# Weights one at a time through all banks, the attention's tenth product behind z2 row 7, and no marking matmuls

## The chip, the cores and the metric

One core of a Trainium2 chip runs the kernel. The metric is device time in microseconds (us), taken as the median of several executions. One further execution was taken with the hardware profiler; rows of the profile come from that one alone.

## The reference

```python
def reference(A_x, A_wqkv, A_wo, B_x, B_w_in, B_w_sp, B_b_sp, B_w_out):
    x = A_x                                   # 1 x 2048 x 512, fp32
    xn = _layernorm(x, axis=-1)
    s = _A_ref(xn, A_wqkv, A_wo)              # attention: 32 heads of 16, window of 8 keys, dilation 2, then @ wo
    g = _silu(_B_ref(xn, B_w_in, B_w_sp, B_b_sp, B_w_out))
    return x + s * g

def _B_ref(x, w_in, w_sp, b_sp, w_out):       # Fh = 896
    z = _gelu(jnp.einsum("bsd,df->bsf", x, w_in))
    z1 = z[..., :Fh]
    z2 = _layernorm(z[..., Fh:], axis=-1)
    g = jnp.einsum("ts,bsf->btf", w_sp, z2) + b_sp[None, :, None]   # w_sp is 2048 x 2048
    return jnp.einsum("bsf,fd->bsd", z1 * g, w_out)
```

## The kernel before

Every fp32 matrix product is made of three matmuls on operands that are split into a high and a low part: high x high, high x low, low x high. A split (`split`, L194) is one copy on ACT (L195, the high part) and one subtraction on DVE (L197, the low part). The 2,048 rows stand in 16 tiles of 128; "row j" below is such a tile.

The stages on TensorE (PE) are, in this order: the qkv product; z1; z2 (`z2_half`, L725, two halves of each row: 512 columns with h = 0 and 384 columns with h = 1, each in a PSUM bank of its own); the mixing product with `w_sp` (`block_product`, L848, in fourteen parts named m1a, m1b, m2a, ... in Strassen's manner, from sums and differences of blocks); the product with `w_out` (L1067 to L1069, tile b); and the product of the attention with `wo` (the same lines, tile s).

A mixing part with the letter a or b runs in one half of the eight PSUM banks: `banks[0, f]` for a, `banks[1, f]` for b, with three or four banks f each. It runs over eight weight blocks s. For a bank and a block, `three` (L823) issues three matmuls of 512 columns. Blocks are taken in pairs: within a pair, bank 0 takes its three matmuls of block s0 and its three of block s0 + 1, then bank 1 takes the same two blocks, and so on. The weights (`wsp_...` from `w_sp`, `ws_...` from sums that were stored before) are loaded into one of four raw buffers, and split into one of eight pairs of weight buffers. m1a uses z2 rows 0 to 7 as the stationary operand, m1b the same rows, and m2a and m2b use rows 8 to 15.

The first parts, m1a and m1b, are not opened by a matmul that overwrites. ACT writes a bias into each bank first (`seed`, L842) and the matmuls add to it. For that, the whole bank has to have been marked as written by a matmul. The banks of m1a were last used by 512-column halves of z2. Those of m1b, `banks[1, f]`, were last used by the 384-column halves of rows 6, 14, 7 and 15; so `second_seeds` (L981) first issues four 512-column matmuls that mark them (L984), one for each bank, and then the four seeds. It is called after blocks 4 and 5 of m1a.

z2 rows come in pairs i and i + 8. After both halves of both rows have gone through Gelu on ACT (L733), `z2_stats` (L738) takes their statistics (DVE L742, L743 and L745, then POOL L746 and L748), and `z2_normal` (L752) normalises a row on ACT (L754) and splits it. `combine` (L759) makes differences and sums of a row pair on DVE (L767), splits one and stores the others. Rows 7 and 15 are the last pair.

DVE also carries the whole attention, in one fixed order (`line`, L537): 32 steps, each with a score product (L573), a reduction (L580), a weighted product (L620, collected in `sums_of`) and some folds (L638 to L646); a first fold runs on POOL (L633). Its output goes to memory (`o_d`), and `load_o` (L803) reads it back for the last stage, in four groups of four tiles (o_0 to o_3).

The order of the instructions on each engine is made ahead of time by a scheduler that simulates the run; every engine then works strictly in that order. Manual dependencies that add no wait (NOSYNC) only constrain that order. One such holds `sums_of[9]`, the tenth weighted product, behind the low part of weight block 6 of m1a (L864); as the attention is one line, all that follows it there waits too.

Of the kernel before, what the change touches and what calls it, by code (L numbers as in the profile page):

```python
# [13 lines left out]
AF = mybir.ActivationFunctionType  # L14
# [5 lines left out]
FH = F // 2  # L20
FQ = FH // 2
H, DH, W, DIL = 32, 16, 8, 2
NT = S // P
# [3 lines left out]
CT = 512  # L27
NC = S // CT
JC = NT // NC
HT = NT // 2  # L30
F3 = 3 * P
ODD = 3
# [20 lines left out]
NOSYNC = mybir.DependencyInfo(mybir.DependencyClass.NoSync, mybir.DependencyReason.DATA)  # L53
# [4 lines left out]
def kernel(  # L58
# [13 lines left out]
    nc = tc.nc  # L72
    pins = [True]
    lows, highs, sums_of = [], [], []

    def pin(ins):
        return tc.keep_in_program_order(ins) if pins[0] else ins
# [35 lines left out]
    mvz = const.tile([P, NT, 2], F32, name="mvz")  # L113
    nmz = const.tile([P, NT], F32, name="nmz")
# [5 lines left out]
    def xn_at(j):  # L120
        return planes[:, FB - KB :, j, 0], planes[:, FB - KB :, j, 1]

    def z2_at(j):
        return planes[:, :, j, 0], planes[:, :, j, 1]

    def half(i):
        return BIG[:, i * CT : (i + 1) * CT]
# [16 lines left out]
    def blocks(t, n=KB):  # L144
        return t.rearrange("p (k q) -> p k q", k=n)
# [9 lines left out]
    def mm(name):  # L155
        return ps.tile([P, 512], F32, tag=f"bank{next(turn)}", name=name)
# [3 lines left out]
    def weight_pair(name):  # L160
        i = next(slot)
        return (
            wts.tile([P, 512], F32R, tag=f"whi{i}", name=name + "h"),
            wts.tile([P, 512], F32R, tag=f"wlo{i}", name=name + "l"),
        )

    def fetch(src, n, name):
        raw = raws.tile([P, 512], F32, tag="raw", name=name + "r", bufs=RAW)
        pin(nc.sync.dma_start(raw[:, :n], src))
        return raw  # L170

    def side_pair(name):
        return [wts.tile([P, CT], F32R, tag=f"w{n}", name=name + n) for n in "hl"]

    def prep(src, n, name, raw=None, pair_=None):
        if raw is None:
            raw = fetch(src, n, name)
        hi, lo = pair_ or weight_pair(name)
        split(hi[:, :n], lo[:, :n], raw[:, :n])
        return hi, lo  # L180
# [13 lines left out]
    def split(hi, lo, src):  # L194
        first_ = pin(nc.scalar.activation(hi, src, AF.Copy))  # L195
        highs.append(first_)
        lows.append(pin(nc.vector.tensor_tensor(lo, src, hi.bitcast(F32), op=ALU.subtract)))  # L197
        return first_
# [48 lines left out]
    rows = {}  # L247
# [45 lines left out]
    first = []  # L293
# [401 lines left out]
    for f in range(FB):  # L695
        pair_ = side_pair("w1_last") if f == FB - 1 else None
        wh, wl = prep(w_in1[:, f, :], KB * P, f"w1_{f}", pair_=pair_)
        for c in range(NC):
            pz = mm(f"z1_{f}_{c}")
            for k in range(KB):  # L700
                cc = slice(k * P, (k + 1) * P)
                xh, xl = [planes[:, FB - KB + k, c * JC : (c + 1) * JC, a] for a in range(2)]
# [5 lines left out]
            zt = zp[:, c % 2]  # L708
# [8 lines left out]
    HALF = (slice(0, 512), slice(512, FH))  # L717
    WID = (512, FH - 512)
    w2 = {
        (k, h): prep(w_in2[:, k, HALF[h]], WID[h], f"w2_{k}_{h}")  # L720
        for h in range(2)
        for k in range(KB)
    }

    def z2_half(j, h, zt):  # L725
        xh, xl = xn_at(j)
        pz = mm(f"z2_{j}_{h}")[:, : WID[h]]
        for k in range(KB):
            wh, wl = [w[:, : WID[h]] for w in w2[k, h]]
            nc.tensor.matmul(pz, xh[:, k], wh, start=k == 0, stop=False)  # L730
            nc.tensor.matmul(pz, xh[:, k], wl, start=False, stop=False)  # L731
            nc.tensor.matmul(pz, xl[:, k], wh, start=False, stop=k == KB - 1)  # L732
        nc.scalar.activation(zt[:, HALF[h]], pz, AF.Gelu_apprx_tanh)  # L733

    def spatial_block(c, js):
        return prep(w_sp[c, js], CT, f"wsp_{c}_{js}")
# [14 lines left out]

    def z2_normal(j, zt, n):  # L752
        zh, zl = z2_at(j)
        nc.scalar.activation(zt, zt, AF.Identity, bias=nmz[:, j : j + 1], scale=mvz[:, j, 1:2])  # L754
        split(zh[:, :n], zl[:, :n], blocks(zt, FB)[:, :n])

    first_part, last_part = slice(0, F3), slice(FH - F3, FH)

# [19 lines left out]
    spatial = {(0, 0): early_pair}  # L778
    raw_z = {}
    for i in range(HT + 2):  # L780
        if i in (1, 3):
            raw_sums(1, HT - 2 + i // 2)
        if i < HT:
            raw_z[i] = [t4(f"zt_{j}").rearrange("p i t -> p (i t)")[:, :FH] for j in (i, HT + i)]
            for h in range(2):
                for j, zt in zip((i, HT + i), raw_z[i]):
                    z2_half(j, h, zt)
                if i == HT - 1 and h == 0:
                    spatial[0, 1] = spatial_block(0, 1)
        if i == 5:  # L790
            b_a = t4("b_a")
            nc.sync.dma_start(
                b_a, b_sp[0:2, :].rearrange("c t -> (c t)").unsqueeze(0).to_broadcast([P, 2 * CT])
            )
            biases = [[b_a[:, 0], b_a[:, 1]]]
        if 0 < i <= HT:
            z2_stats(i - 1, raw_z[i - 1])
        if i > 1:
            for j, zt, n in zip((i - 2, HT + i - 2), raw_z[i - 2], (ODD + 1, FB)):
                z2_normal(j, zt, n)  # L800
            combine(i - 2, raw_z[i - 2])
# [21 lines left out]
    def three(pg, z, w, start=False, stop=False, seeded=False):  # L823
        for i, (a, b) in enumerate(((0, 0), (0, 1), (1, 0))):
            nc.tensor.matmul(  # L825
                pg, z[a], w[b], start=start and i == 0, stop=stop and i == 2, skip_group_check=seeded
            )

    def z2_block(j, f):
        return [planes[:, f, j, a] for a in range(2)]  # L830
# [6 lines left out]
    banks = {}  # L837
    for n in range(8):
        a, f = n // 2 % 2, n // 4 * 2 + n % 2
        banks[a, f] = mm(f"g_{a}_{f}")  # L840

    def seed(a, f, src, scale=1.0):  # L842
        return nc.scalar.activation(banks[a, f], src, AF.Copy, scale=scale)
# [3 lines left out]

    def block_product(a, name, z, w, odd=None, start=False, stop=False, steps=()):  # L848
        for n, s0 in enumerate(range(0, HT, 2)):
            pair_ = [(s, w(s)) for s in (s0, s0 + 1)]  # L850
            for f in range(ODD):
                for s, wp in pair_:
                    three(banks[a, f], z(s, f), wp, start and s == 0, s == HT - 1, not start)
            if odd:
                for s, wp in pair_:
                    three(banks[a, ODD], odd(s), wp, False, s == HT - 1, True)
            for do in steps[n] if steps else ():
                do()

    def plain(a, c, r):  # L860
        def w(s):
            js = r * HT + s
            pair_ = spatial.get((2 * a + c, js)) or spatial_block(2 * a + c, js)
            if (a, c, js) == (0, 0, 6):  # L864
                tc.add_manual_dep(
                    sums_of[9].ins, lows[-1].ins.name, NOSYNC, reason="first weights ahead"
                )
            return pair_

        return w  # L870

# [17 lines left out]
    def odd(r):  # L889
        return lambda s: z2_block(r * HT + s, ODD)  # L890
# [88 lines left out]
            nc.sync.dma_start(biases[1][i], b_sp[2 + i : 3 + i, :].to_broadcast([P, CT]))  # L979

    def second_seeds():  # L981
        for f in range(ODD + 1):

            nc.tensor.matmul(  # L984
                banks[1, f], z2_block(0, f)[0], half(0), start=True, stop=True
            )
        for f in range(ODD + 1):
            seed(1, f, biases[1][0])

    block_product(  # L990
        0, "m1a", at(0, 0), plain(0, 0, 0), odd(0),
        steps=(
# [6 lines left out]
    def kept(a):  # L999
# [7 lines left out]

    kept(0)
    block_product(1, "m1b", at(0, 0), plain(1, 0, 0), odd(0))
    kept(1)  # L1010
    block_product(
        0, "m2a", at(1, 0), plain(0, 0, 1), odd(1),
        steps=([T3[0]], [T3[1]], [T3[2]], [T3[3]]),
# [59 lines left out]
    for i, j in enumerate(rows_of):  # L1073
        c, jj = divmod(j, JC)
# [104 lines left out]
```

## Time and profile before

| | |
|---|---|
| median of 3 executions | 695.06 us (694.0 to 696.38) |
| the profiled execution | 696.54 us |
| its span, first to last instruction | 694.8 us |
| PE busy | 686.6 us (99%) |
| DVE busy | 619.4 us (89%) |
| ACT busy | 277.7 us (40%) |
| POOL busy | 215.2 us (31%) |

A busy PE is not PE at its peak: matmuls overlap, so one lasts 389 ns while the next starts earlier. The start-to-start distance is what counts. 1.74 us of the profiled execution lie outside its span.

### The profile page before, as it was taken

The page shows a single profiled execution, that of the slowest core. Times are in us where ns is not written, and L with a number is a line of the kernel's source. Part 1 is how long each engine was busy: PE and PEld are TensorE (multiplying, and loading weights), DVE is VectorE, ACT ScalarE, POOL GpSimd, SP SyncE. Part 2 cuts the span into 40 slices and gives each one's busy share as a digit, 9 for nine tenths or more (in the row PEclk, how much of TensorE's full clock was granted, in tenths as well). Part 3 has the DMA queues.
Part 4 walks back from the last instruction along what each step waited for, and adds up shares of the span by engine and source line. Part 5 has one row for each costly group of instructions (what it writes and reads, how often), then busy time and mean ns, then how long its engine had stood idle before and what let it go on. Part 6 is the DMA issues. An engine that isn't in the chain of part 4 may idle for free.

```text
span 694.8 us, 9233 instructions
## 1 busy us (share of the span) xinstructions
PE 686.6 (99%) x3084; PEld 573.0 (82%) x3084; DVE 619.4 (89%) x866; ACT 277.7 (40%) x458; POOL 215.2 (31%) x242
## 2 busy tenths in 40 slices
PE   8999999999999999998999999999999999999998
PEld 7888888888888899986888888888888888888886
DVE  6776868999989989889999998999989999989775
ACT  4342234224424256865534544442334444211531
POOL 3104837372343322124123222223111201642320
PEclk9999999999999999999999999999999999999999
DMA  8769899969999865267899768667576692655796
GB/s 270 252 193 289 288 348 384 346 204 358 407 412 340 329 231 190 80 201 231 258 403 314 284 211 298 208 232 248 183 261 206 215 342 89 221 173 190 246 330 235
DMA packets 102223, 182.36 MB, mean 262 GB/s; under 512 B 9184, under 2 KB 45280, under 8 KB 102176
## 3 DMA queue, kind: packets, MB, share of 16 engines
q1 hardware_dynamic: 56624, 102.21, 43.6%
q0 software_dynamic: 13824, 52.24, 20.9%
q10 hardware_dynamic: 31728, 27.33, 11.7%
q8 instruction: 24, 0.39, 0.2%
q14 instruction: 23, 0.19, 0.1%
HBM read 122.42 MB, written 59.32 MB: 262 GB/s over the span
## 4 chain that ended last, share of the span: by engine, by line
PE 67%; DVE 13%; DMA 12%; ACT 3%; issue 3%; POOL 1%; SPq 1%; DVEq 0%; POOLq 0%; ACTq 0%
PE g L825 35%; PE b L1067 4%; PE b L1069 4%; PE b L1068 4%; PE qkv L387 4%; PE qkv L386 4%; PE qkv L385 4%; DMA sb<-in_w_sp 3%; PE s L1069 2%; PE s L1068 2%; PE s L1067 2%; DMA sums_d<-sb 2%; DVE zst L742 2%; DMA z_d<-z1t 1%; DVE xT L280 1%
## 5 line engine op out<-in xcount | busy, mean ns | idle before, releaser
L633 POOL TENSOR_TENSOR pv<-pv 128x1024 f32<-128x1024 f32 x29 | 69.6, 2399 | 96.2 <-DVE pv L620 85.9
L573 DVE TENSOR_TENSOR pr<-k,q 128x2048 f32<-128x2048 f32 x32 | 73.6, 2299 | 2.0 <-DMA k<-qkv_d 1.9
L620 DVE TENSOR_TENSOR pv<-v,lg 128x2048 f32<-128x2048 f32 x32 | 74.6, 2331 | 0.7
L580 DVE TENSOR_REDUCE lg<-pr 128x128 f32<-128x2048 f32 x32 | 73.0, 2281 | 0.1
L647 POOL DMA_DIRECT2D o_d<-tt x32 | 18.0, 562 | 138.9 <-DVE tt L646 103.8
L433 ACT ACTIVATE stage<-qkv 128x512 f32<-128x512 f32 x40 | 23.0, 590 | 30.8 <-DMA qkv_d<-stage 17.0
L807 POOL DMA_DIRECT2D ol<-o_d x32 | 17.7, 555 | 37.7 <-DVE BIG L197 11.1
L1078 ACT ACTIVATE bt<-b 128x512 f32<-128x512 f32 x16 | 9.4, 599 | 43.5 <-PE b L1069 39.4
L709 ACT ACTIVATE z1t<-z 128x512 f32<-128x512 f32 x28 | 15.5, 597 | 26.1 <-DMA z_d<-z1t 15.3
L280 DVE TENSOR_TENSOR xT<-xT,mr 128x512 f32<-128x512 f32 x20 | 14.9, 743 | 11.9 <-DMA mr<-mv_d 6.4
L732 PE MATMUL z<-w_0h,BIG 128*128 128x512 f32 x64 | 25.0, 391 | 0.0
L731 PE MATMUL z<-w_0l,BIG 128*128 128x512 f32 x64 | 25.0, 391 | 0.0
L730 PE MATMUL z<-w_0h,BIG 128*128 128x512 f32 x64 | 24.9, 390 | 0.0
L742 DVE BATCH_NORM_STATS2 zst<-zt 128x6 f32<-128x448 f32 x32 | 19.3, 613 | 6.1 <-ACT zt L733 6.0
L754 ACT ACTIVATE zt<-zt,nmz,mvz 128x896 f32<-128x896 f32 x16 | 17.5, 1129 | 18.0 <-POOL nmz L748 18.0
L638 DVE TENSOR_TENSOR pv<-pv 128x512 f32<-128x512 f32 x32 | 22.9, 716 | 0.0
L733 ACT ACTIVATE zt<-z 128x512 f32<-128x512 f32 (+1 forms) x32 | 15.9, 536 | 15.2 <-DMA sums_d<-sa 14.0
L732 PE MATMUL z<-w_1h,BIG 128*128 128x384 f32 x64 | 21.5, 336 | 0.0
L730 PE MATMUL z<-w_1h,BIG 128*128 128x384 f32 x64 | 21.5, 335 | 0.0
L731 PE MATMUL z<-w_1l,BIG 128*128 128x384 f32 x64 | 21.4, 335 | 0.0
L393 POOL TENSOR_TENSOR sb<-sa,sb 128x512 f32<-128x512 f32 x12 | 19.7, 1644 | 5.4 <-DMA sb<-in_w_sp 5.1
L195 ACT ACTIVATE BIG<-zl 128x512 fp32r<-128x512 f32 x20 | 12.5, 630 | 21.6 <-DVE zl L895 19.8
(478 smaller groups left out, 2296.2 us busy)
## 6 DMA issues: line engine op xcount, KB each, us to landing
qkv_d<-stage ACTq DMA_DIRECT2D x24, 512.0 KB
v<-qkv_d POOLq DMA_DIRECT2D x14, 704.0 KB, 5.4
k<-qkv_d POOLq DMA_DIRECT2D x13, 704.0 KB, 6.8
sums_d<-sa POOLq DMA_DIRECT2D x14, 512.0 KB, 7.8
sums_d<-sb POOLq DMA_DIRECT2D x14, 512.0 KB, 8.0
z_d<-z1t ACTq DMA_DIRECT2D x14, 512.0 KB
zl<-z_d SPq DMA_DIRECT2D x12, 512.0 KB
tr<-t_d SPq DMA_DIRECT2D x12, 384.0 KB
```

The lines of the kernel that those rows point to most:

```text
L573: line(nc.vector.tensor_tensor(pr, taps(ks[u], j0), qb.unsqueeze(1).to_broadcast([P, W, NJ * CS]), op=ALU.mult))
L580: line(nc.vector.tensor_reduce(lgs[u][:, j0 * HS : (j0 + NJ) * HS].rearrange("p i w -> p w i"), pr.rearrange("p w (i d) -> p w i d", d=DH) ...
L620: line(nc.vector.tensor_tensor(pv.rearrange("p w (i d) -> p w i d", d=DH), taps(vs[u], j0).rearrange("p w (i d) -> p w i d", d=DH), lgs[u] ...
L633: eng.tensor_tensor(pv[:, 0:4], pv[:, 0:4], pv[:, 4:8], op=ALU.add)
L730: nc.tensor.matmul(pz, xh[:, k], wh, start=k == 0, stop=False)
L731: nc.tensor.matmul(pz, xh[:, k], wl, start=False, stop=False)
L732: nc.tensor.matmul(pz, xl[:, k], wh, start=False, stop=k == KB - 1)
L742: nc.vector.bn_stats(st[:, h], zt[:, h * FQ : (h + 1) * FQ])
L825: nc.tensor.matmul(pg, z[a], w[b], start=start and i == 0, stop=stop and i == 2, skip_group_check=seeded)
L1067: nc.tensor.matmul(pp[:, cols], hi, wh, start=k == 0, stop=False)
L1068: nc.tensor.matmul(pp[:, cols], hi, wl, start=False, stop=False)
L1069: nc.tensor.matmul(pp[:, cols], lo, wh, start=False, stop=k == n - 1)
```

## The change

- `block_product` takes the weight blocks one at a time: for each block s, all banks get their three matmuls before the next block begins. The number and the kinds of matmuls stay the same.
- `second_seeds` loses its four marking matmuls. In their place the first matmul of the 384-column half of rows 6, 7, 14 and 15 writes all 512 columns of its bank. For this the first weight block of that half (`w2_0_1`) is loaded and split with 512 columns instead of 384, the half's result stands in the last 384 columns of its bank, and the other matmuls remain 384 wide.
- The order constraint on `sums_of[9]` moves from the low part of weight block 6 of m1a to the low part of z2 row 7.
- A new order constraint on ACT puts the normalisation of row 15 behind the high part of row 7.

```diff
@@ w2 and z2_half
     w2 = {
-        (k, h): prep(w_in2[:, k, HALF[h]], WID[h], f"w2_{k}_{h}")
+        (k, h): prep(
+            w_in2[:, k, slice(FH - CT, FH) if (k, h) == (0, 1) else HALF[h]],
+            CT if (k, h) == (0, 1) else WID[h],
+            f"w2_{k}_{h}",
+        )
         for h in range(2)
         for k in range(KB)
     }
 
     def z2_half(j, h, zt):
         xh, xl = xn_at(j)
-        pz = mm(f"z2_{j}_{h}")[:, : WID[h]]
+        bank = mm(f"z2_{j}_{h}")
+        pz = bank[:, CT - WID[h] :]
         for k in range(KB):
-            wh, wl = [w[:, : WID[h]] for w in w2[k, h]]
-            nc.tensor.matmul(pz, xh[:, k], wh, start=k == 0, stop=False)
+            wh, wl = [w[:, CT - WID[h] :] if k == 0 else w[:, : WID[h]] for w in w2[k, h]]
+            if k == 0 and j % HT >= HT - 2:
+                nc.tensor.matmul(bank, xh[:, k], w2[k, h][0], start=True, stop=False)
+            else:
+                nc.tensor.matmul(pz, xh[:, k], wh, start=k == 0, stop=False)
             nc.tensor.matmul(pz, xh[:, k], wl, start=False, stop=False)
             nc.tensor.matmul(pz, xl[:, k], wh, start=False, stop=k == KB - 1)
@@ z2_normal
-        nc.scalar.activation(zt, zt, AF.Identity, bias=nmz[:, j : j + 1], scale=mvz[:, j, 1:2])
+        ins = nc.scalar.activation(zt, zt, AF.Identity, bias=nmz[:, j : j + 1], scale=mvz[:, j, 1:2])
+        if j == NT - 1:
+            tc.add_manual_dep(ins.ins, highs[-1].ins.name, NOSYNC, reason="first products' row ahead")
         split(zh[:, :n], zl[:, :n], blocks(zt, FB)[:, :n])
+        if j == HT - 1:
+            tc.add_manual_dep(sums_of[9].ins, lows[-1].ins.name, NOSYNC, reason="gate rows ahead")
@@ block_product
         for n, s0 in enumerate(range(0, HT, 2)):
-            pair_ = [(s, w(s)) for s in (s0, s0 + 1)]
-            for f in range(ODD):
-                for s, wp in pair_:
+            for s in (s0, s0 + 1):
+                wp = w(s)
+                for f in range(ODD):
                     three(banks[a, f], z(s, f), wp, start and s == 0, s == HT - 1, not start)
-            if odd:
-                for s, wp in pair_:
+                if odd:
                     three(banks[a, ODD], odd(s), wp, False, s == HT - 1, True)
@@ plain
-            pair_ = spatial.get((2 * a + c, js)) or spatial_block(2 * a + c, js)
-            if (a, c, js) == (0, 0, 6):
-                tc.add_manual_dep(
-                    sums_of[9].ins, lows[-1].ins.name, NOSYNC, reason="first weights ahead"
-                )
-            return pair_
+            return spatial.get((2 * a + c, js)) or spatial_block(2 * a + c, js)
@@ second_seeds
         for f in range(ODD + 1):
-
-            nc.tensor.matmul(
-                banks[1, f], z2_block(0, f)[0], half(0), start=True, stop=True
-            )
-        for f in range(ODD + 1):
             seed(1, f, biases[1][0])
```

## Rows read from the trace of the kernel before

**Rows 1.** The page: busy time by engine; granted clock in 40 slices, tenths of full.

```profile
PE 686.6 (99%) x3084; PEld 573.0 (82%) x3084; DVE 619.4 (89%) x866; ACT 277.7 (40%) x458; POOL 215.2 (31%) x242
...
PEclk9999999999999999999999999999999999999999
```

**Rows 2.** Busy us by stage: stretch, length, PE, PEld, DVE, ACT, POOL, clock, DMA, GB/s.

```profile
295.13:342.27 47.14, 45.03 (x197) 36.59 (x197) 44.87 (x70) 28.00 (x47) 12.77 (x14) 1.00 0.70 221
342.27:570.94 228.67, 228.67 (x1010) 189.35 (x1009) 220.94 (x300) 94.39 (x156) 52.41 (x51) 1.00 0.76 262
```

**Rows 3.** PE's waits between 290 and 330 us: total, times, longest.

```profile
PE g L825 <- ACT g L843: 1.9, 1, 1.9
PE g L825 <- ACT BIG L195: 0.2, 1, 0.2
```

**Rows 4.** PE in order of time, m1a and m1b: start, duration, engine, line, operation.

```profile
290.94 0.33 PE L730 MATMUL z<-w_1h,BIG 128*128 128x384 f32 x1
...
295.13 0.39 PE L825 MATMUL g<-wsp_0h,BIG 128*128 128x512 f32 x1
...
311.49 1.07 PE L984 MATMUL g<-BIG 128*128 128x512 f32 x4
312.39 0.39 PE L825 MATMUL g<-wsp_6h,BIG 128*128 128x512 f32 x1
...
317.17 0.50 PE L825 MATMUL g<-wsp_0h,BIG 128*128 128x512 f32 x1 [1.90 <-ACT g L843]
...
324.48 0.50 PE L825 MATMUL g<-wsp_7h,BIG 128*128 128x512 f32 x1 [0.21 <-ACT BIG L195]
...
342.30 0.39 PE L825 MATMUL g<-wsp_8h,BIG 128*128 128x512 f32 x1
```

**Rows 5.** ACT in order of time: last Gelu, m1b's seeds, rows 7 and 15.

```profile
303.82 0.47 ACT L733 ACTIVATE zt<-z 128x384 f32<-128x384 f32 x1
...
313.99 0.64 ACT L195 ACTIVATE wsp_3h<-wsp_3r 128x512 fp32r<-128x512 f32 x1 [5.03 <-DMA wsp_3r<-in_w_sp]
...
316.53 2.14 ACT L843 ACTIVATE g<-b_bh 128x512 f32<-128x512 f32 x4
321.22 2.16 ACT L754 ACTIVATE zt<-zt,nmz,mvz 128x896 f32<-128x896 f32 x2 [2.54 <-POOL nmz L748]
...
323.81 1.88 ACT L195 ACTIVATE BIG<-zt 128x512 fp32r<-128x512 f32 x3
```

**Rows 6.** DVE in order of time: attention between row 7's steps.

```profile
304.04 2.29 DVE L620 TENSOR_TENSOR pv<-v,lg 128x2048 f32<-128x2048 f32 x1
306.24 2.28 DVE L580 TENSOR_REDUCE lg<-pr 128x128 f32<-128x2048 f32 x1
...
309.29 0.62 DVE L742 BATCH_NORM_STATS2 zst<-zt 128x6 f32<-128x448 f32 x1
...
313.22 2.28 DVE L573 TENSOR_TENSOR pr<-k,q 128x2048 f32<-128x2048 f32 x1
...
327.36 2.15 DVE L197 TENSOR_TENSOR BIG<-zt,BIG 128x512 fp32r<-128x512 f32 x3
```

**Rows 7.** POOL in order of time: the reciprocal root for rows 7 and 15.

```profile
318.82 1.68 POOL L746 TENSOR_TENSOR mvz<-mvz,nhalf 128x2 f32<-128x2 f32 x1 [1.83 <-DVE mvz L745]
```

**Rows 8.** DVE's longest waits between 350 and 660 us: total, times, longest.

```profile
DVE ws_4l L197 <- ACT ws_4h L195: 3.6, 2, 2.3
DVE o_0l L197 <- ACT o_0h L195: 2.2, 1, 2.2
```

**Rows 9.** The attention's last tile: its low part on DVE, its first use on PE.

```profile
679.59 0.69 DVE L197 TENSOR_TENSOR o_3l<-ol,o_3h 128x512 fp32r<-128x512 f32 x1 [3.30 <-ACT o_3h L195]
...
682.07 0.39 PE L1069 MATMUL s<-BIG,o_3l 128*128 128x512 f32 x1
```

**Rows 10.** The weight block with the shortest lead: low part, first use.

```profile
392.05 0.68 DVE L197 TENSOR_TENSOR ws_5l<-ws_5r,ws_5h 128x512 fp32r<-128x512 f32 x1
...
395.33 0.39 PE L825 MATMUL g<-ws_5l,BIG 128*128 128x512 f32 x1
```

## The prediction

> **What bounds the kernel now.** I read the page first: TensorE (PE) is busy for 686.6 of 694.8 us, and its granted clock is full in each of the 40 slices [rows 1]. So the time is that of PE's stream of matmuls and its gaps, and only removed matmuls or closed gaps can count. Next I looked for the gaps by stage. From 342 to 571 us PE is busy for the whole stretch: 1,010 matmuls in 228.67 us, 0.2264 us each [rows 2]. That is the price of a dense 512-column matmul. The stretch before it, m1a with m1b, has 2.1 us in which PE is idle [rows 2]. Then the waits: PE waits twice here, 1.9 us for the seeds of m1b and 0.2 us for a high part of z2 [rows 3]. Last, the order of the matmuls around these waits [rows 4]: after block 6 of m1a PE does not go on to block 7, which needs row 7. It waits for m1b's seeds and begins m1b, and comes back to block 7 at 324.48. So row 7 is late, and the seeds that would fill in for it are late too.
>
> Why they are late is seen on the other engines. The last Gelu of rows 7 and 15 is done at 304.29 [rows 5]. Then DVE takes up the attention at 304.04: the tenth weighted product, the reduction, a score product (2.3 us each) and folds [rows 6]. Row 7's statistics stand between these (309.29), POOL has its root at 320.5 [rows 7], ACT normalises rows 7 and 15 from 321.22 and copies from 323.81 [rows 5], and the low parts come from 327.36 [rows 6]. The seeds ran at 316.53, four microseconds after the marking matmuls on which they wait. They stood on ACT behind copies of m1b's later weights, one of which waited 5 us for its transfer [rows 5].
>
> **What the dense stream would give.** From 295.13 to 342.30, 47.17 us, PE issues 192 weighted and four marking matmuls [rows 4]. At 0.2264 these take 44.4. So the two waits cost **2.8 us**: 2.1 idle, and the rest around them, as a matmul after a wait lasts 0.50 instead of 0.39 and the next one starts later [rows 4].
>
> **Part by part.**
> - *The marking matmuls go.* Four, from 311.49 to 312.39: **0.90 us** off PE's stream [rows 4]. The seeds lose their wait for PE; they then need only the Gelu that empties the last bank (304.29 [rows 5]) and the bias.
> - *Narrow halves wider.* The last 24 narrow matmuls take 290.94 to 295.13, 0.175 us each [rows 4]; a wide one takes 0.226. Four of them: **0.2 us** added to the stream. The wider first weight adds about a third to one load, one copy and one subtraction early in z2; a 512-column copy and subtraction last 0.64 and 0.68 us in all [rows 5, 10]. PE does not wait there; without that cover it would be below 0.2 us.
> - *The tenth product behind row 7's low part.* DVE is in order, so everything of the attention waits with it; POOL's fold and the loads of the next keys, queries and values wait for those in turn. Row 7's chain after its last Gelu: statistics 0.62 [rows 6], POOL's root 1.68 [rows 7], one normalisation (half of 2.16) and one copy (a third of 1.88) [rows 5], one subtraction 0.7 [rows 6]; with some 1.1 for the small steps between them (an estimate from POOL's 320.50 and ACT's 321.22 [rows 5, 7], 0.7 for one handover, and a little for the other) that is 5.8 us, so 310.1 at the earliest. At the latest: from 304.04 to the low parts at 327.36 are 23.3 us, and DVE is hardly idle (44.87 of 47.14 us busy [rows 2]). Five large attention steps lie in it, the three shown and one more product and reduction of the same length, 11.4 us [rows 6]; all the rest, 11.9 us at most and with wsp_6's low part among it, done first would end near 315.2, when that 0.7 is taken off. PE needs row 7's high part after 84 dense matmuls from 295.13, at 314.2, and its low part two matmuls later, at 314.6. So the cost of what is left of the wait lies between 0 and 0.6 us. I take 0.3, as the late end assumes that the scheduler lets nothing of row 7 go ahead.
> - *What DVE loses.* The work that goes ahead is work that stood between the attention's steps anyway, so the attention is moved, not lengthened, by as much as DVE idles for row 7's chain: between 0 and 5.8 us, were there nothing else to do. I take 1, as some 11 us of other work lie there.
> - *Row 15 behind row 7.* In the trace ACT normalises both rows in one go, then copies [rows 5]. Now row 7's copy goes between: 1.1 us earlier for row 7, 0.6 later for row 15, which is first used by block 7 of m2a, over 40 us on. Nothing.
> - *One block at a time.* The same matmuls. An odd block is needed nine matmuls later than before with four banks (2.0 us), an even block's buffer is free nine earlier. The shortest lead that I found between a low part and its use is 2.6 us (392.73 to 395.33 [rows 10]); this order lengthens leads. Against it: m1b's second to fourth bank are needed three matmuls (0.68 us) after one another instead of six; four seeds take 2.14, or 0.53 each [rows 5], so they keep up. At the end of a part the first bank is complete 9 instead of 18 matmuls ahead, but the next part works in the other four banks, so 72 or 96 matmuls, 16 to 22 us, pass before it is needed. Nothing.
>
> Sum: 0.9 - 0.2 + 2.8 - 0.3 = 3.2; I take **3.1 us**, leaving 0.1 for the restart. The ceiling is 0.9 - 0.2 + 2.8 = 3.5. The profiled execution of 696.54 (span 694.8 and 1.74 around it) would become 693.4. It lies 1.5 above the median of 695.06, and for the median I forecast **692.0 us**.
>
> **A rule against the reordering.** The row first: through 342 to 571 us PE changed banks every six matmuls, some 170 times, with no idle time at a granted clock of 1.00, the 2.4 GHz level [rows 2]. The Trainium skill, "TensorE: Matmul & The Clock Gate", section "A second HAM failure mode: psum-queue depth-cycling", tells of a kernel that cycled through banks and had so many tiny idle times between groups that the clock fell back again and again; by that rule three matmuls a bank would cost time in all fourteen parts. The trace so far speaks against it. It is the last rival below.
>
> **The rivals.**
> 1. *The attention becomes the end.* The low part of the attention's last tile is done at 680.28 and used at 682.07: 1.8 us to spare [rows 9]. If PE comes 3.1 us earlier and the attention does not, 1.3 us are given back: 693.3. For it: DVE is 97% busy from 342 to 571 [rows 2]. Against: DVE waits for ACT later on, 5.8 us in three waits alone [rows 8], on copies that wait for buffers or queues that PE frees; those waits absorb a DVE that is late.
> 2. *Row 7 isn't what it waits for, or the scheduler places it as late as before.* Then only the markers count, 0.9 - 0.2: 694.4. For it: what else stood between the Gelu and the root on DVE. Against: the attention's share of that stretch is half of it.
> 3. *Slower: the attention starts too late and nothing absorbs it.* If DVE idles through all of row 7's chain, the tenth product begins at 310.1 instead of 304.04, and if the later waits are set by transfers, the last tile comes 5.8 us later: 1.8 are spare, so the end moves by 4.0, to 699.1. It decides from a slip of 1.8 us plus what the waits of [rows 8] absorb (5.8): below 1.8 never, above 7.6 always.
> 4. *The clock falls with the bank changes.* No row here has the lower level; were a tenth of the 1,200 weighted matmuls to take twice 0.2264, it would be 27 us more: 722.
>
> **How the numbers follow.** Forecast 0.54 (691.0 to 692.9; it includes a gain at the ceiling); attention at the end 0.16 (692.6 to 694.3); no cure for row 7 0.11 (694.4); attention far too late 0.16 (696 to 699); the clock 0.02; an unrelated change of the scheduler's order for the worse 0.01. A measurement of this kernel can tell about 0.3%, 2.1 us, from no change: below 692.97 is faster, above 697.15 slower. The forecast and a tenth of the first rival's higher gains give faster 0.56; the rest of rivals 1 and 2 and the mild half of rival 3 make 0.32; slower 0.12. The range 690.8 to 696.6 leaves out the worse part of rival 3 and the clock; its low end is the ceiling (691.6) less the 0.8 by which a median of such runs can lie low.
>
> **What would show it.** Right: no marking matmuls; PE without a wait from 295 to about 338.8, where m2a begins (342.3 minus 3.5); block 7 of m1a directly behind block 6, row 7's copy on ACT before 314; the seeds of m1b on ACT before 314; the tenth product right behind row 7's low part at 309 to 315; the last tile's low part about 3 us earlier; DVE's later waits shorter. Wrong: PE waiting for `o_` parts after 640 (rivals 1 and 3), a wait for a high part of z2 (rival 2), or a granted clock below 1.00 (rival 4). The sum would be wrong from its start if the scheduler's order in the stages behind m2a brought PE new waits where it has none today.

## The result: 0.33% slower, and where the time went

The changed kernel takes 698.22 us in the median (693.67 to 702.03, 22 runs), the kernel before 695.95 us in the same series (694.0 to 698.45, 22 runs). The ratio is 1.0033, with a 95% interval of [1.0018, 1.0047]: slower by a little, but clear of the noise, where 692.0 us and faster was forecast. The profiled execution of the changed kernel took 698.9 us, with a span of 697.0.

These are the two lines of the changed kernel's page that answer to [rows 1]. PE is as busy as before with four matmuls fewer, and the granted clock is still full.

```profile
PE 686.5 (98%) x3080; PEld 571.7 (82%) x3080; DVE 619.6 (89%) x866; ACT 275.9 (40%) x458; POOL 214.7 (31%) x242
PEclk9999999999999999999999999999999999999999
```

Stage windows of the changed kernel (columns as in [rows 2]): m1a with m1b, which had 2.1 us of idle PE before, is dense now. The stretch from 500 to 580 us, part of a stretch without any idle time before, has lost 3.9 us.

```profile
295.20:342.30 47.10, 47.04 (x208) 38.62 (x207) 41.93 (x67) 28.60 (x49) 11.43 (x12) 1.00 0.71 222
342.30:500.00 157.70, 157.70 (x697) 130.59 (x696) 150.05 (x196) 60.02 (x102) 40.46 (x39) 1.00 0.76 261
500.00:580.00 80.00, 76.13 (x331) 61.29 (x330) 77.01 (x112) 32.84 (x56) 12.58 (x13) 1.00 0.72 238
```

PE's waits in the changed kernel (line, what released it: total, times, longest), those behind the start. The two of [rows 3] are gone; three new ones stand in the last mixing part and the output product, for weights:

```profile
PE g L837 <- DVE ws_0l L197: 1.8, 1, 1.8
PE b L1068 <- ACT wout_5h L195: 1.2, 1, 1.2
PE b L1069 <- DVE wout_2l L197: 0.8, 1, 0.8
```

The order around row 7 is what was asked for. ACT, then DVE, in order of time: the seeds run at 307.58 instead of 316.53 [rows 5], row 7 has its high part at 313.14, DVE its low part at 313.88, and the tenth product comes right behind, at 314.48 instead of 304.04 [rows 6].

```profile
307.58 2.16 ACT L855 ACTIVATE g<-b_bh 128x512 f32<-128x512 f32 x4 [1.25 <-DMA b_bh<-in_b_sp]
...
311.58 1.14 ACT L762 ACTIVATE zt<-zt,nmz,mvz 128x896 f32<-128x896 f32 x1 [0.87 <-POOL nmz L756]
...
313.14 0.62 ACT L195 ACTIVATE BIG<-zt 128x512 fp32r<-128x512 f32 x1
```

```profile
313.27 0.69 DVE L197 TENSOR_TENSOR wsp_3l<-wsp_3r,wsp_3h 128x512 fp32r<-128x512 f32 x1 [1.31 <-ACT wsp_3h L195]
313.88 0.68 DVE L197 TENSOR_TENSOR BIG<-zt,BIG 128x512 fp32r<-128x512 f32 x1
314.48 2.28 DVE L620 TENSOR_TENSOR pv<-v,lg 128x2048 f32<-128x2048 f32 x1
```

The largest of the new waits, first on PE, then on DVE, then on ACT. PE has its high part and waits for the low part of ws_0. ACT had made the high part from 530.67 on, so neither the transfer nor ACT is late. DVE had it right behind the 23rd product and its reduction in its order, 4.4 us of work, and reached it at 536.53. In the kernel before the 23rd product ran at 523.34; here at 532.13.

```profile
535.38 0.39 PE L837 MATMUL g<-ws_0h,BIG 128*128 128x512 f32 x1
537.53 0.50 PE L837 MATMUL g<-ws_0l,BIG 128*128 128x512 f32 x1 [1.76 <-DVE ws_0l L197]
```

```profile
532.13 2.28 DVE L620 TENSOR_TENSOR pv<-v,lg 128x2048 f32<-128x2048 f32 x1
534.33 2.27 DVE L580 TENSOR_REDUCE lg<-pr 128x128 f32<-128x2048 f32 x1
536.53 0.95 DVE L197 TENSOR_TENSOR ws_0l<-ws_0r,ws_0h 128x512 fp32r<-128x512 f32 x1
```

```profile
530.67 0.64 ACT L195 ACTIVATE ws_0h<-ws_0r 128x512 fp32r<-128x512 f32 x1 [1.71 <-DMA ws_0r<-sums_d]
```

The same low part and its first use in the kernel before: done at 532.20, used at 538.36, a lead of 6.2 us. In the changed kernel DVE is done with it 5.3 us later (537.48), and PE would have used it 2.6 us earlier (537.53 less the wait of 1.76). Together that is 7.9 us: the lead is used up, and 1.7 us of wait remain.

```profile
531.53 0.67 DVE L197 TENSOR_TENSOR ws_0l<-ws_0r,ws_0h 128x512 fp32r<-128x512 f32 x1
...
538.36 0.39 PE L825 MATMUL g<-ws_0l,BIG 128*128 128x512 f32 x1
```

Of the other two waits, that for wout_2 is for a low part on DVE as well; that for wout_5 is for a high part on ACT, which had waited for that block's transfer.

DVE also lost time between row 7 and these waits. At 432.80 it waits 3.4 us for the high part of a stored row difference (`tr`), for whose transfer ACT had waited 3.9 us; in the second execution of the changed kernel DVE waits 3.1 us there. None of the three executions of the kernel before has this wait. Why the transfer comes late is open. ACT, then DVE:

```profile
431.92 0.85 ACT L195 ACTIVATE BIG<-tr 128x768 fp32r<-128x768 f32 x1 [3.92 <-DMA tr<-t_d]
```

```profile
432.80 0.96 DVE L197 TENSOR_TENSOR BIG<-tr,BIG 128x768 fp32r<-128x768 f32 x1 [3.42 <-ACT BIG L195]
```

Three profiled executions of the kernel before and two of the changed one (the further ones are experiments below) put this into one table. It is made from the starts of three matmuls on PE: the first of m1a, the first of m2a, the last of all.

| execution | m1a and m1b, us | m2a to the last matmul, us | together |
|---|---|---|---|
| before | 47.17 | 348.72 | 395.89 |
| before, second | 45.14 | 348.72 | 393.86 |
| before, third | 45.30 | 348.72 | 394.02 |
| changed | 43.91 | 354.15 | 398.06 |
| changed, second | 43.69 | 352.97 | 396.66 |

From m2a on, the kernel before takes the same 348.72 us three times: nothing makes its PE wait there. The changed kernel gains 1.2 to 3.5 us in m1a and m1b and loses 4.3 to 5.4 us behind them. The means differ by 2.8 us, the medians by 2.3.

### The profile page after: what moved, and what is told of

Same layout as the page of the kernel before. It is cut to its first block, busy times and chain, and to the rows that moved or that the text cites. A ratio compares the mean times of both kernels' runs of the same rounds, so it can differ in the third digit from the quotient of the medians.

```text
span 697.0 us, 9227 instructions
## 1 busy us (share of the span) xinstructions
PE 686.5 (98%) x3080; PEld 571.7 (82%) x3080; DVE 619.6 (89%) x866; ACT 275.9 (40%) x458; POOL 214.7 (31%) x242
## 4 chain that ended last, share of the span: by engine, by line
DVE 33%; PE 31%; DMA 17%; issue 13%; ACT 2%; POOL 1%; SPq 1%; DVEq 0%; ACTq 0%; POOLq 0%
DVE lg L580 5%; DVE pr L573 5%; PE qkv L385 4%; PE qkv L386 4%; PE qkv L387 4%; PE b L1068 3%; PE b L1070 3%; PE b L1069 3%; DVE BIG L197 3%; DMA tr<-t_d 3%; DVE pv L620 3%; PE s L1070 2%; PE s L1069 2%; PE s L1068 2%; DMA sums_d<-sb 2%
## 5 line engine op out<-in xcount | busy, mean ns | idle before, releaser
L740 PE MATMUL z<-w_0h,BIG 128*128 128x512 f32 x64 | 25.0, 391 | 0.0
L754 POOL TENSOR_TENSOR mvz<-mvz,nhalf 128x2 f32<-128x2 f32 x8 | 7.6, 944 | 51.3 <-DVE mvz L753 51.3
L738 PE MATMUL z<-w_0h,BIG 128*128 128x512 f32 x60 | 23.3, 389 | 0.0
L740 PE MATMUL z<-w_1h,BIG 128*128 128x384 f32 x64 | 21.5, 336 | 0.0
L552 POOL DMA_DIRECT2D k<-qkv_d x13 | 7.0, 536 | 44.5 <-DVE pr L573 44.5
```

## The experiments

The first four undo one part of the change, do one part alone, or take work off DVE. "Idle" below is DVE's idle time from 295 to 340 us: 2.3 us in the first execution of the kernel before (0.9 in each of the other two), 5.2 and 4.7 in the two of the changed kernel.

**Block pairs again (a_pairs).** The changed kernel with its blocks in pairs.

```diff
-            for s in (s0, s0 + 1):
-                wp = w(s)
-                for f in range(ODD):
+            pair_ = [(s, w(s)) for s in (s0, s0 + 1)]
+            for f in range(ODD):
+                for s, wp in pair_:
```

> The changed kernel with the weight blocks of block_product taken in pairs again; all else as changed. Theory (the attention, held behind row 7, leaves DVE with a backlog, and low parts of weights come late to PE): the order of the blocks is not the cause, so the tenth product still starts near 314 us, PE still waits 2 to 5 us for low parts between 500 and 580, and the time is 1.003 of before, near 698. Rival (taking blocks one at a time makes the scheduler put the weights' low parts later on DVE): no PE wait after 500 us, and 692 to 693.5.

Measured: 1.0014 [0.9992, 1.0036]; idle 4.1; no wait from 500 to 580 us in its profile. The shortest lead of a low part there is 1.4 us, where the changed kernel has leads of 0.0 to 0.4 at nine blocks. The late waits that the theory expected are gone, but the time of the rival isn't reached either. The profile suggests that the order of the blocks has a share in the loss together with the rest; the times do not show it, as this interval overlaps that of the changed kernel.

**The constraint back at weight block 6 (a_dep6).** The changed kernel without the hold behind row 7; row 15 stays behind row 7.

```diff
-        if j == HT - 1:
-            tc.add_manual_dep(sums_of[9].ins, lows[-1].ins.name, NOSYNC, reason="gate rows ahead")
+            if (a, c, js) == (0, 0, 6):
+                tc.add_manual_dep(sums_of[9].ins, lows[-1].ins.name, NOSYNC, reason="first weights ahead")
```

> The changed kernel with the constraint on the tenth weighted product moved back to weight block 6 of m1a; blocks one at a time, no marking matmuls and row 15 behind row 7 as changed. Theory (backlog of DVE from the held attention): the tenth product is back near 304 us, row 7 is late again and PE waits 1 to 3 us near 315 to 325, but under 0.5 us between 500 and 580; the time is 694 to 695.5, about 1 below before. Rival (order of the blocks): waits of 2 us or more between 500 and 580 stay, and the time is 697 to 699.

Measured: 1.0015 [0.9994, 1.0036]; idle 2.0, the tenth product at 302.5; row 7 costs PE only 0.26 us, but there are waits of 1.1 us for ws_6's low part at 395, 0.5 for wout_3's and 1.0 for o_3. Neither expectation holds: PE isn't held at row 7, and the gain of 1 us is not there.

**Single blocks alone (b_single).** The kernel before with only the new block order.

```diff
-            pair_ = [(s, w(s)) for s in (s0, s0 + 1)]
-            for f in range(ODD):
-                for s, wp in pair_:
+            for s in (s0, s0 + 1):
+                wp = w(s)
+                for f in range(ODD):
```

> The kernel before with one part of the change alone: weight blocks one at a time. Theory (backlog of DVE): no new wait after 330 us, within 0.3% of before, 694 to 697. Rival (order of the blocks): 2 to 5 us of new PE waits for low parts after 500 us, 698 to 701.

Measured: 1.0001 [0.9983, 1.0018]; idle 0.9; after 295 us PE waits only once, 0.3 us for o_3. By itself the new order neither gains nor costs. That the new order makes the late waits by itself is refuted.

**A lighter DVE (a_light).** The changed kernel with the reduction of steps 15 to 26 taken over half of each head's elements, about 13 us less on DVE.

```diff
-                pr.rearrange("p w (i d) -> p w i d", d=DH),
+                pr.rearrange("p w (i d) -> p w i d", d=DH)[:, :, :, : DH // 2 if 14 <= 2 * u + j0 // NJ < 26 else DH],
```

> The changed kernel with less work on DVE: in twelve of the attention's 32 steps (the 15th to the 26th) the reduction sums only half of each head, so 1.1 us is saved in each, 13 us in all (the scores of these steps are then partial sums). Theory (backlog of DVE): PE's waits between 500 and 580 shrink from 5 us to under 0.5, and the time is 691.5 to 693. Rival (order of the blocks, or anything on ACT or the transfers): the waits stay within a microsecond of 5, and the time is above 696.5.

Measured: 1.0045 [1.0024, 1.0065], no cure. The tenth product came at 315.2, idle was 6.7, and PE waited 1.8 us for ws_1's low part at 522. The windows from 430 to 565 us, of a_light and then of the changed kernel, show what happened: with 13 us less to do DVE was busier in this stretch (third of the engines' figures), not idler. The scheduler had made the order anew, moved the attention forward (the 23rd product at 507.8 us instead of 532.1), and left the low parts just in time, with leads of 0.0 to 1.3 us at twelve blocks from 500 to 580.

```profile
430.00:565.00 135.00, 133.23 (x588) 109.78 (x587) 134.27 (x186) 48.86 (x84) 30.02 (x28) 1.00 0.66 231
```

```profile
430.00:565.00 135.00, 133.15 (x586) 109.51 (x585) 128.79 (x175) 51.36 (x87) 28.41 (x26) 1.00 0.67 224
```

So less work alone is no cure, as the order changes with it. What was left to test: DVE's order is fixed ahead, and time that it loses around row 7 comes due later, where low parts are made just before their use.

**The hold a little earlier (a_ts).** The tenth product waits for row 7's last statistics operation on DVE.

```diff
+        ins = nc.vector.tensor_scalar(rstd, rstd, EPS, None, op0=ALU.add)
+        if i == HT - 1:
+            tc.add_manual_dep(sums_of[9].ins, ins.ins.name, NOSYNC, reason="statistics ahead")
...
-        if j == HT - 1:
-            tc.add_manual_dep(sums_of[9].ins, lows[-1].ins.name, NOSYNC, reason="gate rows ahead")
```

> The changed kernel, but the tenth attention product waits on VectorE for the last statistics operation of z2 row 7 instead of that row's low part. Theory (VectorE's order is fixed ahead; idle time that the plan did not foresee at 295 to 340 us, plus TensorE's lead, makes low parts come late against their use at 500 to 580): the product goes at 308 to 311 us (314.5 in the changed kernel), VectorE's idle time of 295 to 340 falls from 5.2 to 2 to 3.5 us, TensorE's lost time at 500 to 580 from about 5.2 to at most 2.5 us, and the time is 695 to 696.8, ratio 0.999 to 1.002. Rival (only the new block order and the lighter marks are at fault, not where the product waits): the lost time at 500 to 580 stays at 4 to 6 us and the ratio at 1.002 to 1.005.

Measured: 1.0002 [0.9988, 1.0016], the product at 310.9, no loss from 500 to 580 us, as the theory had it. Idle, however, was 4.4, not 2 to 3.5 (1.4 of it a transfer of the bias). PE's waits and its window:

```profile
PE g L837 <- DVE BIG L197: 1.4, 1, 1.4
PE g L837 <- ACT g L855: 0.7, 1, 0.7
PE g L837 <- ACT BIG L195: 0.5, 1, 0.5
```

```profile
500.00:580.00 80.00, 80.00 (x355) 66.24 (x354) 78.27 (x117) 33.22 (x57) 12.58 (x13) 1.00 0.75 254
```

PE now waits for row 7 again, 47.0 us from m1a to m2a: nothing is gained there and nothing lost later. What spares the later blocks isn't separated by this run. PE begins m2a 3.5 us later than in the changed kernel (342.65), and DVE has its 23rd product 7.3 us earlier (524.84).

**Two low parts pulled ahead (a_hold).** The changed kernel, with the 23rd product held behind the low part of the next weight block and the 24th behind wout_3's.

```diff
+    holds = {(0, 1, 0, 1): 22}
+                tc.add_manual_dep(sums_of[holds[a, half_, i, s]].ins, lows[-1].ins.name, NOSYNC, reason="weights ahead")
+        if f == 3:
+            tc.add_manual_dep(sums_of[23].ins, lows[-1].ins.name, NOSYNC, reason="weights ahead")
```

> The changed kernel, with two attention products more held on VectorE behind low parts: the one that stood ahead of the late block at 535 us, and the next one behind the low part of wout_3. Theory (the stalls at 535 and 571 to 577 us are VectorE's order and nothing else): the waits for ws_0 and for wout low parts, 2.0 and 2.8 us in the profile of the changed kernel, fall to under 1 us in all, and the output phase starts 2 to 4 us earlier against the dense sum; the time is 693.5 to 696, ratio 0.998 to 1.001, unless the attention's end then comes late, which would show as waits for o_ tiles after 640 us. Rival (the weights' transfers or ScalarE's high parts are late): the waits stay and go to high parts or to transfers, ratio 1.002 to 1.005.

Measured: 1.0082 [1.0057, 1.0106]. Both expectations missed the time; the late o_ tiles are the exception that the theory had named. The wait for ws_0 vanished, one for wout_4 stayed, and the attention's last tile, now held back, became the longest:

```profile
PE s L1082 <- ACT o_3h L195: 3.6, 2, 2.8
PE b L1083 <- DVE wout_4l L197: 1.8, 1, 1.8
PE b L1082 <- ACT wout_4h L195: 0.3, 1, 0.3
```

Here the time that DVE had lost was moved from the weights to the attention's end, not removed.

**The marking matmuls alone (b_marks)** and **with single blocks (bs_marks, bs_marks_2).** The kernel before with the `w2` and `z2_half` part of the change and the marking loop out; in bs_marks also the diff of b_single. No constraint of the change.

```diff
-        for f in range(ODD + 1):
-            nc.tensor.matmul(banks[1, f], z2_block(0, f)[0], half(0), start=True, stop=True)
```

> The kernel before with the marking matmuls taken out and the four k = 0 halves made 512 wide, nothing else. Four matmuls of 0.23 us less and some 0.2 us more: 0.7 us less by the sum, ratio 0.997 to 1.000, if the order of the other engines stays. If the scheduler's order moves with it, VectorE's waits of 350 to 660 us show it, and the time can come out up to 1.5 us above.

> The kernel before with blocks one by one and the marking matmuls gone and halves wider, but with the tenth product still behind weight block 6, and row 15 free. Theory (each of the edits alone does no harm; the wait for row 7's low part is what spends VectorE's lead): VectorE's idle time of 295 to 340 us is 0.5 to 2.5 us, TensorE loses under 1 us at 500 to 580, and the time is 693.5 to 695.5, ratio 0.997 to 1.000. Rival (the block order with the marks gone is enough to make low parts late): waits for ws_ and wout_ low parts of 2 us or more, ratio 1.001 to 1.004.

> bs_marks once more, as the base of bs_delay on the same chip and to narrow its interval: ratio 0.998 to 1.0003, no wait over 0.5 us on TensorE after 300 us.

Measured: b_marks 1.0005 [0.9987, 1.0023], with a wait of PE of 1.2 us for row 7's high part; bs_marks 0.9992 [0.998, 1.0003], and in a later series 0.9991 [0.998, 1.0003]. bs_marks has no wait on PE behind the start in its first profile and one of 0.2 us in the second; from m1a to the last matmul it takes 392.44 and 393.39 us. Its windows:

```profile
295.00:342.10 47.10, 47.10 (x208) 38.77 (x208) 45.93 (x69) 29.17 (x50) 13.35 (x14) 1.00 0.73 234
...
500.00:580.00 80.00, 80.00 (x355) 66.24 (x354) 78.28 (x114) 34.14 (x58) 13.26 (x13) 1.00 0.71 247
```

This is the best kernel of the study, 0.4% under the changed one, and still inside what can be told from the kernel before.

**Row 15 free (a_row15).** The changed kernel without the constraint on row 15's normalisation.

```diff
-        if j == NT - 1:
-            tc.add_manual_dep(ins.ins, highs[-1].ins.name, NOSYNC, reason="first products' row ahead")
```

> The changed kernel without the order that puts row 15's normalisation on ScalarE behind row 7's high part; the tenth product still waits for row 7's low part. Theory (the product's wait and VectorE's idle time are what cost): the time stays near that of the changed kernel, ratio 1.001 to 1.004, with VectorE idle for 3.5 to 6 us at 295 to 340 us. Rival (the order of row 15 has a price of its own on ScalarE and VectorE, which the kernel with the constraint back at weight block 6 kept): ratio 0.998 to 1.000 and under 2 us lost on TensorE at 500 to 580.

Measured: 1.0223 [1.0196, 1.025], beyond both expectations. The tenth product went at 317.5 and idle was 9.7 us, for these reasons first (DVE's waits from 295 to 340 us), with these waits of PE:

```profile
DVE wsp_10l L197 <- ACT wsp_10h L195: 3.5, 1, 3.5
DVE zst L750 <- ACT zt L741: 2.7, 1, 2.7
DVE wsp_3l L197 <- ACT wsp_3h L195: 1.4, 1, 1.4
```

```profile
PE s L1066 <- ACT o_3h L195: 4.3, 1, 4.3
PE g L835 <- DVE ws_3l L197: 3.2, 1, 3.2
PE g L835 <- ACT BIG L195: 0.7, 1, 0.7
```

**The kernels unchanged, once more (before_2, before_3, after_2).** One profiled execution each.

> The kernel before, unchanged: a second profiled execution. Theory (the two waits of 2.05 and 0.37 us at 314.9 and 323.9 us are planned and come in every execution): the multiply-accumulate stages m1a and m1b lose 2 to 3 us again and the span is 694 to 695. Rival (they belong to that one execution): they lose under 1 us and the span is 692 to 693.5.

> The kernel before, unchanged: a third profiled execution, with the same two expectations as the second: 2 to 3 us lost on TensorE at 314 to 325 us and a span of 694 to 695, or under 1 us and 692 to 693.5.

> The changed kernel, unchanged: a second profiled execution. Theory (the late stalls come with the kernel): TensorE runs without a stall over 0.5 us at 300 to 350 us, and loses 3 to 7 us at 500 to 580 us to low parts of ws_ and wout_; span 695 to 699. Rival (they belong to that one execution): under 1.5 us lost there, span 691 to 693.

Measured: spans of 692.4, 694.2 and 695.1 us; the table above has the rest. The late waits come again in the second execution of the changed kernel. The early ones of the kernel before do not come again: PE loses 0.54 and 0.75 us from 314 to 325 us, where the first execution loses 2.63. The third execution has a span of 694.2 all the same, as m1a begins only at 296.40 in it (294.85 in the second). What differed in the first is one transfer. ACT in the first execution, then in the second:

```profile
302.76 0.63 ACT L195 ACTIVATE wsp_6h<-wsp_6r 128x512 fp32r<-128x512 f32 x1 [1.48 <-DMA wsp_6r<-in_w_sp]
```

```profile
300.39 0.62 ACT L195 ACTIVATE wsp_6h<-wsp_6r 128x512 fp32r<-128x512 f32 x1
...
318.91 2.17 ACT L754 ACTIVATE zt<-zt,nmz,mvz 128x896 f32<-128x896 f32 x2 [2.62 <-POOL nmz L748]
```

The raw weight block wsp_6 landed late in the first one. Its low part on DVE was late by that, the tenth product behind it went at 304.04 instead of 301.74, and with it everything in DVE's line, row 7's statistics too: the normalisation began at 321.22 [rows 5] instead of 318.91.

**The two constraints alone (b_dep7).** The kernel before, block pairs and marking matmuls kept, with the row 7 and row 15 constraints of the change.

```diff
+        if j == NT - 1:
+            tc.add_manual_dep(ins.ins, highs[-1].ins.name, NOSYNC, reason="first products' row ahead")
+        if j == HT - 1:
+            tc.add_manual_dep(sums_of[9].ins, lows[-1].ins.name, NOSYNC, reason="gate rows ahead")
-            if (a, c, js) == (0, 0, 6):
-                tc.add_manual_dep(sums_of[9].ins, lows[-1].ins.name, NOSYNC, reason="first weights ahead")
```

> The kernel before with the two constraints of the change alone: the tenth product behind row 7's low part in place of weight block 6, and row 15's normalisation behind row 7's high part; blocks in pairs and marking matmuls as before. Theory (the product's hold costs by itself): VectorE idle 3.5 to 6 us at 295 to 340 us, the tenth product at 312 to 316 us, waits for ws_ or wout_ low parts or o_ tiles of 1.5 us or more in all, ratio 1.0015 to 1.005. Rival (it costs only together with the new block order): ratio 0.999 to 1.001 and waits under 1 us.

Measured: 1.0026 [1.0009, 1.0043], idle 6.0, the tenth product at 312.5: the theory. Most of the loss of the changed kernel is there without its block order and without its matmul changes. PE's waits:

```profile
PE g L829 <- DVE ws_7l L197: 1.1, 1, 1.1
PE b L1066 <- ACT wout_4h L195: 1.0, 1, 1.0
PE g L829 <- ACT g L847: 0.5, 1, 0.5
```

**Extra work on DVE (bs_delay).** bs_marks, with the tenth product made three times, 4.6 us more.

```diff
             sums_of.append(last[-1])
+            for _ in range(2 * (len(sums_of) == 10)):
+                line(nc.vector.tensor_tensor(
...
+                    op=ALU.mult,
+                ))
```

> The kernel with single blocks and without marking matmuls, tenth product behind weight block 6 (bs_marks), in which that product is computed three times over: 2 x 2.28 = 4.6 us of extra work on VectorE, which the scheduler counts with when it fixes the order. Theory of capacity (whatever VectorE loses around 300 to 320 us comes due at 500 to 580 us or at the o_ tiles): 2 us or more of new waits on TensorE there, ratio to before 1.001 to 1.005. Theory of the unplanned (only lost time that the planned order did not count with comes due): waits under 1 us in all, ratio 0.998 to 1.000, as bs_marks.

Measured: 1.0242 [1.0219, 1.0265]; its base bs_marks_2 in the same series 0.9991. The theory of the unplanned is refuted: work that the planned order counts with comes due too. The theory of capacity has the sign, but the size is far beyond what it expected, and the place is only one of the two named: nothing is lost from 500 to 580 us, all of it at row 7 and at the end. Behind the last matmul the span goes on for 8.6 us, 3.7 in bs_marks_2, as DVE still has late tiles to finish.

```profile
PE s L1078 <- ACT o_3h L195: 5.8, 1, 5.8
PE g L842 <- ACT BIG L195: 2.3, 1, 2.3
PE s L1078 <- DVE sg L1139: 2.0, 1, 2.0
```

The eleventh product came at 332.6 us, 12.7 later than in bs_marks_2 (319.9), with DVE idle for 2.9 us instead of 1.2: other work stood between. Why 4.6 us of work move it by 12.7 is open, and so is how the scheduler shares a loss between weights and attention. Also open is a price of row 15's constraint: a_dep6 and bs_marks differ in it alone and lie 0.23% apart, but their intervals overlap.

## Why the prediction was wrong, point by point

- **PE's own stream: right.** m2a starts at 339.14 us; 338.8 was forecast. 43.91 us from m1a to m2a are 192 dense matmuls and one new stall of 0.35 at 297.1, where the fourth bank's seed is needed three matmuls after the third's. The marking matmuls, the seeds before 314, row 7's copy before 314 and a product at 309 to 315 all came as said, with no wait at row 7.
- **The 2.8 us of the two waits: mis-sized.** It was read off one execution in which one weight block landed late. Two further executions of the kernel before show 0.54 and 0.75 us lost around the two waits, and 45.14 and 45.30 us for the stages; against these the change gains 1.2 to 1.6 us there and not 3.1. The term of 2.8 is some 0.8 to 0.9 in them (196 dense matmuls take 44.4). The profiled execution lay 1.5 us above the median, which the prediction noted and then took off as a constant. From m1a on that execution is 1.9 to 2.0 us longer than the two others, all of it in the stages where the prediction found its gain: the wait was counted twice, once as a gain and once in those 1.5 us.
- **"What DVE loses", taken as 1 us between 0 and 5.8: mis-sized, and not all of it is lost at row 7.** Idle rises by 2.4 to 2.9 us from the first execution of the kernel before, by 3.8 to 4.3 from the others, which lies within the bounds. But DVE then loses time once more, in the wait at 432.80 shown above. From 295 to 530 us DVE is idle for 9.7, 7.2 and 7.8 us in the kernel before and for 13.8 and 12.5 in the changed one. Over all profiles this figure goes with the waits of PE behind m2a: up to 10.0 us (the kernel before, b_single, b_marks, bs_marks, bs_marks_2, a_ts) these are 0.3 us or less, from 10.7 (a_pairs) to 18.2 (a_row15) they are 0.4 to 7.8 in all. The exception is a_light, with 9.6 and other work on DVE. That is one profile for each, and shows that the two go together, not more. The attention is moved by more than the idle time: the tenth product comes 10.4 us later than in the first execution of the kernel before, the 23rd 8.8 and the last of the list 3.6 us later.
- **The step that turned the sign: that DVE's later waits absorb what it loses, so that it costs nothing in the sum.** The waits of [rows 8] did shrink, from 3.6 and 2.2 us to 1.6 and 0.5. But the new wait for `tr` came in their place, and the waits of [rows 8] do not lie ahead of every low part that PE needs. The prediction's shortest lead, 2.6 us [rows 10], belongs to another place; ws_0 near 535 us had 6.2 us. A DVE that was 5.3 us late there met a PE that was 2.6 us early, and the lead was gone. Behind m2a the changed kernel lost 4.3 to 5.4 us that the sum had at nothing, more than the gain ahead of it.
- **"One block at a time lengthens leads": not borne out.** b_single comes out at 1.0001; its shortest lead behind m2a is 1.9 us, where the three executions of the kernel before have 2.6, 3.3 and 2.2. Whether the order has a share in the loss of the changed kernel is not shown by the times (a_pairs).
- **"Row 15: nothing": wrong where it stands with the other constraint.** Without it the changed kernel is 1.9% slower still (a_row15, 1.0223 against 1.0033). Nor did the prediction ask what each constraint does without the other; the four kernels with single blocks and no marking matmuls answer:

| | product behind weight block 6 | product behind row 7 |
|---|---|---|
| row 15 free | 0.9992, 0.9991 | 1.0223 |
| row 15 behind row 7 | 1.0015 | 1.0033 |

- **The rivals.** The third, "the attention starts too late and nothing absorbs it", came nearest to the mechanism and, with 699.1, to the time, at 0.16. That its time fits is in part luck: it put the price at the last tile, where the changed kernel waits for nothing (the low part of o_3 comes at 682.83, 3.2 us later than in [rows 9], as PE does); the price was paid at weights, over 100 us earlier. In a_hold, a_row15 and bs_delay most of it is paid at the last tile. The first and second did not happen. The fourth did not either: three matmuls a bank ran at a granted clock of 1.00 in every window above, and no idle time came with the bank changes (157.70 of 157.70 us busy from 342.30 to 500). The Trainium skill, "TensorE: Matmul & The Clock Gate", section "A second HAM failure mode: psum-queue depth-cycling", tells of small idle times between groups of matmuls, with which the clock goes back and forth. The trace has no such idle times there, so that rule had nothing to act on.
- **What the prediction named as a sign of its own error came true:** new waits of PE in the stages behind m2a. Its chance for an order that turns out worse was 0.01, though it knew DVE to be 97% busy there [rows 2].

## What to carry to other kernels

A wait that is to be gained has to be seen in more than one execution: compare the stage's length, not one wait, before it enters a sum. Where an in-order engine is some 97% busy for hundreds of microseconds, an edit that holds it for row data early can be paid far behind it, so list the leads on that engine over the whole span behind the edit, and set them against the time that it loses plus the time that the consumer gains. Count its idle time over the whole span too, and not only at the edit. In a_hold, pulling the late items ahead by more constraints moved the loss to what was pushed back.

## What the hardware showed that was not expected

A long wait of PE costs more than itself. In a_row15 PE waited 3.2 us at 408 us; before it the granted clock was 1.00, and in the 4 us behind it 0.58, with matmuls 0.43 us apart instead of 0.227, the 1.2 GHz level. The stretch of the wait, then the one behind it (the clock is the third last figure):

```profile
407.80:411.30 3.50, 0.34 (x2) 0.00 (x0) 3.50 (x4) 2.09 (x4) 2.35 (x1) 1.00 0.23 88
411.30:415.30 4.00, 3.95 (x10) 3.15 (x11) 4.00 (x11) 0.63 (x1) 0.00 (x0) 0.58 0.93 315
```

The waits of 4.35 us at the end of a_row15, 5.75 in bs_delay and 2.80 in a_hold were followed by the same spacing of 0.43 us. Those of 1.8 us in the changed kernel and 2.3 in bs_delay were not. This is part of why a_row15 and bs_delay lose far more than DVE's lost time. And one transfer of a weight block, late by some 2 us in one execution, made the kernel before longer by about as much (395.89 us from m1a to the last matmul against 393.86 and 394.02), although PE itself did not wait for that block.
